# Gated linear attention into a routed expert layer on one core: fewer two-part sums, and the hand-over of PSUM banks and row gathers to the experts

## The chip, the cores and the metric

The kernel runs on one core of a Trainium2 chip. A core has TensorE (PE, matmuls; its weight loads are listed apart as PEld), VectorE (DVE), ScalarE (ACT), GpSimd (POOL) and SyncE (SP), which work beside one another and wait for each other by semaphores, and 16 DMA engines. The metric is the device time of one execution in microseconds (us). Lower is better. The kernel's arithmetic is f32, with the exception of some sums that are told of below.

## The reference

First a recurrent attention with a decay per key channel, for 4 batches, 8 heads, 768 steps, 48 channels a head. Its result, one row of 384 numbers per step and batch (3072 rows), goes to a layer of eight experts, where each row goes to the one expert with the largest logit.

```python
def _attn_ref(q, k, v, alpha):
    for t in range(S):
        state = alpha[:, :, t, :, None] * state + np.einsum('bhd,bhe->bhde', k[:, :, t], v[:, :, t])
        y[:, :, t] = np.einsum('bhd,bhde->bhe', q[:, :, t], state)

def _moe_ref(x, w_gate, w1, w2):          # x: 3072 x 384, w1: 8 x 384 x 1024, w2: 8 x 1024 x 384
    logits = x @ w_gate
    expert_idx = np.argmax(logits, axis=1)
    ...
    for e in range(E):
        lo, hi = (boundaries[e], boundaries[e + 1])
        h = np.maximum(x_sorted[lo:hi] @ w1[e], 0.0)
        y_sorted[lo:hi] = h @ w2[e]
    y = y_sorted[inv_perm]
    return (gate_w[:, None] * y).astype(np.float32)
```

## The kernel before, in words

**The attention** runs over 24 chunks: 6 stretches of 128 steps for each of 4 batches, numbered so that chunk s is stretch s // 4 of batch s % 4. The main loop (line 703) is a software pipeline with an order written out by hand: in pass i it takes the scores of chunk i, the transposes of chunk i + 1, the operands of chunk i + 2, the result rows of chunk i - 1, the gate of chunk i - 2, and the decay sums of a chunk some five ahead. Each engine works through its instructions in the order in which the program issues them.

For the decay, `logs` takes on ACT the logarithm of alpha (tile `lna`), `cums` sums it over the steps on PE by a product with a triangular matrix (tile `cum` in PSUM), and ACT takes two exponentials of the sum (`icp`, `cp`). The sum is made in one of two ways. Plain: one f32 product with `cum_m`. Two-part, where `apart(s)` holds: `logs` also scales the logarithm into an f16 tile `hi` (ACT), `low_part` puts the remainder into `lo` (DVE), and `cums` adds an f16 and an f32r product. Which pass takes a chunk's logarithm also hangs on the constant APART: from chunk APART on it is taken one pass ahead of the sum, before that in the same pass:

```python
def new_logs(i):
    return [s for j in (i, i + 1) for s in new_sums(j) if (s >= APART) == (j > i)]
```

New sums are those of chunks 4 and 5 in pass 1, 6 and 7 in pass 2, 8 in pass 3, 9 in pass 4, 10 in pass 5 and so on.

In a pass ACT's order is: `yT` (the attention's result out of PSUM), `gex` (gate), the logarithms and scalings, `kT` and for some chunks `qT` (transposed operands), `icp` and `cp`, then `xs` (rows times gate weight, out of the PSUM tile `x`), then the issue of small transfers (`dec`: decay rows of a chunk's first and last step). On POOL each pass forms the operands `kqb` (k times icp, q times cp); every fourth pass it multiplies the decay rows into the tile `er` (lines 445, 446), which PE transposes to `ep` in the next pass (457) for the state's scaling `U` (507). PE's order in a pass is scores, on every fourth pass `ep`, transposes, sum, state and value products, key-value products, rows (`x`).

**The seam.** The experts are worked off by size: places 1 to 7 in order of load, and place 0 for the first expert. Of expert 0's rows the first 256 are gathered and worked early, inside the attention's tail (`early_gather`, `early_layer1`, hidden layer in `eg["h"]`, tile `h0`); the rest, 168 at most, are a group of their own (`groups[0]`), in blocks of 128 and 40. When routing is known (`decode`, `place_experts`, DVE), the attention's pools close, the experts' pools open (line 820 on), and these follow at lines 1229 to 1239: the gather of the rest's rows (two indirect DMAs on POOL), layer 2 of the first early block, `places` (DVE: rows of places 1 to 7), the gather of place 1 (four indirect DMAs), half of layer 2 of the second early block, the transposes of the rest (`turn`), then layer 1 of the rest. `scatter` copies a block of results out of PSUM (ACT, tile `zo`, four buffers) and writes the rows by an indirect DMA on POOL.

PSUM has eight banks of 512 f32 numbers. The attention uses `y` (two banks), `tp` (two), `sA`, `sB`, `cum`, `x`. The experts have a pool `mps` of their own, opened after the attention's pool `ps` has closed: tags `pA`, `pB`, `pC`, `tp`, two buffers each.

**The experts.** Places 1 to 6 run `layer1` and `layer2` in seven products of half size (`chain`): a product goes to a bank, ACT or DVE copies or adds it out. In `layer2`, `p2` writes a `pC` bank, out of which DVE adds, and the product of the third column block goes to the next `pC` bank (line 1025).

Of the kernel before, what the change touches and what calls it, by code (L numbers as in the profile page):

```python
# [20 lines left out]
def kernel(  # L21
# [43 lines left out]
    HC = C // 2  # L65


    APART, HS = 9, 512.0
    assert NB * C == S and FB * C == F and DB * C == Dm and D <= DP


# [20 lines left out]
    cum_r = consts.tile([C, C], F32R)  # L92
    cum_h = consts.tile([C, C], F16)
    kqb = [consts.tile([C, 2, NP, 2, DP], F32, name=f"kqb{i}") for i in range(3)]
    er = consts.tile([C, NP, 2, DP], F32)

    iw = consts.tile([C, NP, D2 + E], F32)

# [133 lines left out]

    sm = ctx.enter_context(tc.tile_pool(name="moe_sm", bufs=1))
    early = ctx.enter_context(tc.tile_pool(name="early", bufs=1))
    oh_r = sm.tile([C, NT, C], F16)
    oh_c = sm.tile([C, NT, NC], F16)

# [121 lines left out]
    def weights(i, layer):  # L359
        if 0 < i < E:  # L360
            ex = nc.sync.value_load(pd["xe"][0:1, i : i + 1], min_val=0, max_val=E - 1)
            groups[i][f"w{layer}"] = fetch(ex, layer)

# [2 lines left out]

    in_order = ExitStack()  # L370
    in_order.enter_context(tc.manual_schedule())
    with tc.tile_pool(name="ld", bufs=6) as ld, \
         tc.tile_pool(name="work", bufs=2) as work, \
         tc.tile_pool(name="ps", bufs=1, space=PSUM) as ps:
        st = {s: {} for s in range(NT)}
        y = ps.tile([C, 2, 512], F32, name="y")
        decay, alpha0 = {}, {}

        def yv(g):
# [13 lines left out]

        def apart(s):

            return s >= APART or s in (5, 7)

        def logs(s):
            t = work.tile([C, Dm], F32, name="lna", bufs=4)
# [412 lines left out]
        early_layer1(FB - 1)  # L812
        d = decode(held["tok"][:], NC, "a")
        g_e = next(d)
        place_experts()
        weights(1, 1)
        _, s_e, gf_e, sf_e = next(d)
# [2 lines left out]
    spool = ctx.enter_context(tc.tile_pool(name="spool", bufs=2))  # L820
    xg_pool = ctx.enter_context(tc.tile_pool(name="moe_x", bufs=2))
    wk = ctx.enter_context(tc.tile_pool(name="moe_wk", bufs=1))
    mps = ctx.enter_context(tc.tile_pool(name="moe_ps", bufs=2, space=PSUM))

    def blocks(g, by=1):
        return [(j, min(C, -(-(g["n"] - j * C) // by) * by)) for j in range(-(-g["n"] // C))]

    def gather(g):
        g["xg"] = xg_pool.tile([C, NJ, Dm], F32, name="xg")
        for j, r in blocks(g, 16):  # L830
            nc.gpsimd.indirect_dma_start(  # L831
                out=g["xg"][:r, j, :], out_offset=None,
                in_=x_d[:, :], in_offset=bass.IndirectOffsetOnAxis(ap=g["gi"](j, r), axis=0),
            )

    def turn(g):
        g["xT"] = wk.tile([C, DB, CAP0 + 8], F32, name="xgT")
        for j, r in blocks(g):
            tp = mps.tile([C, DB, C], F32, name="tp", tag="tp")
            for a in range(DB):  # L840
                nc.tensor.transpose(tp[:, a, :r], g["xg"][:r, j, a * C : (a + 1) * C], ident[:r, :r])
            (nc.scalar.copy if j % 2 else nc.vector.tensor_copy)(g["xT"][:, :, j * C : j * C + r], tp[:, :, :r])
            if j == 1:
                yield
# [32 lines left out]
    def chain(g, terms, out, res):  # L877


        m = g["n"] // 2  # L880
        bank = {}

        def ps(n):
            bank[n] = mps.tile([C, 512], F32, name="p" + n, tag="p" + n)
            return bank[n][:, :m]

        def keep(n):
            t = wk.tile([C, CAP0 // 2], F32, name=n, bufs=2)
            nc.scalar.copy(t[:, :m], bank["A"][:, :m])  # L889
            bank[n] = t  # L890

        def p1():
            terms(ps("A"), True, "P1")
            keep("p1")

        def p2():
            terms(ps("C"), True, "P2", "R11")
            add(nc.vector, out(0, 0), bank["C"][:, :m], bank["p1"][:, :m])
            res(0, 0)

        def p7():
            terms(ps("B"), True, "P7", "R22")

        def p6():
            terms(bank["A"][:, :m], False, "P6")
            keep("u2")

        def p5():
            terms(bank["A"][:, :m], False, "P5")
            keep("u4")  # L910

        def c22():
            add(nc.vector, out(1, 1), bank["B"][:, :m], bank["u4"][:, :m])

        def p3():
            terms(bank["A"][:, :m], False, "P3", "R12")
            res(0, 1, bank["A"][:, :m])

        def p4():
            terms(bank["B"][:, :m], False, "P4", "Rd")  # L920
            add(nc.vector, out(1, 0), bank["B"][:, :m], bank["u2"][:, :m])
            res(1, 0)

        return p1, p2, p7, p6, p5, c22, p3, p4
# [69 lines left out]
    def layer2(g):  # L994
        n, m = g["n"], g["n"] // 2
        w2, h, s, t = g["w2"], g["h"], g["s2"], g["th"]
        g["zT"] = wk.tile([C, DB, CAP0 + 8], F32, name="zT")
        z = g["zT"]
        ops = {}
        for n_, (w, i) in dict(P1=(w2, 0), P2=(w2, FH), P4=(w2, FH), P3=(s, 3), P5=(s, 0), P6=(s, 1), P7=(s, 2)).items():  # L1000
            c0 = C if n_ == "P4" else 0
            for f in range(FH):
                lhs = w2[:, i + f, c0 : c0 + C] if w is w2 else s[:, i, f, :]
                rhs = {
                    "P1": h[:, f, :m], "P2": h[:, FH + f, :m], "P3": h[:, FH + f, m:n],
                    "P4": t[:, 3, f, :m], "P5": t[:, 0, f, :m], "P6": t[:, 1, f, :m], "P7": t[:, 2, f, :m],
                }[n_]
                ops.setdefault(n_, []).append((lhs, rhs))

        def terms(out, first, *names):  # L1010
            for f, (lhs, rhs) in enumerate(ops[names[0]]):
                nc.tensor.matmul(out, lhsT=lhs, rhs=rhs, start=first and f == 0, stop=True, skip_group_check=True)  # L1012

        def out(i, k):
            return z[:, i, k * m : (k + 1) * m]

        def res(i, k, at=None):
            if at is not None:
                nc.scalar.copy(out(i, k), at)

        p1, p2, p7, p6, p5, c22, p3, p4 = chain(g, terms, out, res)

        def rest(ahead, between):
            p2()
            d2 = mps.tile([C, 512], F32, name="pC", tag="pC")

            def third(fs):
                for f in fs:
                    nc.tensor.matmul(  # L1029
                        d2[:, :n], lhsT=w2[:, f, 2 * C :], rhs=h[:, f, :n], start=(f == 0), stop=(f == FB - 1),  # L1030
                    )

            third(range(FH))
            p6()
            next(between)
            third(range(FH, FB))
            ahead()
            nc.scalar.copy(z[:, 2, :n], d2[:, :n])
            next(between)
            p5()  # L1040
            next(between)
            p7()
            c22()
            p3()
            p4()

        return p1, rest
# [44 lines left out]
    def rows_layer2(g, j, fs):  # L1092

        r = min(C, g["n"] - j * C)
        if fs[0] == ready[0]:
            t = "p" + "CAB"[j]
            g["z"] = mps.tile([C, 512], F32, name=t, tag=t)
        for f in fs:
            nc.tensor.matmul(
                g["z"][:r, :Dm], lhsT=g["h"][:, f, j * C : j * C + r], rhs=g["w2"][:, f, :],  # L1100
# [3 lines left out]
    def plain(g):  # L1104

        hT = wk.tile([C, FB, CAP0], F32, name="h_sb")[:, :, :C]
        for f in range(FB):
            hp = mps.tile([C, 512], F32, name="pA", tag="pA")
            for a in range(DB):
                nc.tensor.matmul(  # L1110
                    hp[:, :C], lhsT=g["w1"][:, a, f * C : (f + 1) * C], rhs=g["xT"][:, a, :C],
                    start=(a == 0), stop=(a == DB - 1),
                )
            nc.scalar.activation(hT[:, f, :], hp[:, :C], AF.Relu)
        zp = mps.tile([C, 512], F32, name="pB", tag="pB")
        for f in range(FB):
            nc.tensor.matmul(
                zp[:, :Dm], lhsT=hT[:, f, :], rhs=g["w2"][:, f, :], start=(f == 0), stop=(f == FB - 1),
# [60 lines left out]
        pd.update(xn=xn, xi=xi, xx=xx)  # L1179
        yield  # L1180

    def cols_of(t, c0):
        return lambda j, r: t[:r, c0 + j : c0 + j + 1]

    def early_layer2(j, fs):

        if 0 in fs:
            t = "tp" if j else "pA"
            eg["z"] = mps.tile([C, DB, C], F32, name=t, tag=t).rearrange("p a c -> p (a c)")
        for f in fs:  # L1190
            nc.tensor.matmul(
                eg["z"][:, :Dm], lhsT=eg["h"][:, f, j * C : (j + 1) * C], rhs=groups[0]["w2"][:, f, :],
                start=(f == 0), stop=(f == FB - 1),
            )
        if FB - 1 in fs:
            scatter(eg, j, C, eg["z"][:, :Dm])

    def rest_layer1(g, beside):
        n = g["n"]
        g["h"] = wk.tile([C, FB, CAP0], F32, name="h_sb")  # L1200
        for f in range(FB):
            t = "p" + "CBA"[f % 3]
            hp = mps.tile([C, 512], F32, name=t, tag=t)
            for a in range(DB):
                nc.tensor.matmul(
                    hp[:, :n], lhsT=g["w1"][:, a, f * C : (f + 1) * C], rhs=g["xT"][:, a, :n],
# [8 lines left out]
    def rest_layer2(g, d):  # L1215
        n = g["n"]
        if d == 0:
            g["zT"] = wk.tile([C, DB, CAP0 + 8], F32, name="zT")
        zp = mps.tile([C, 512], F32, name="pA", tag="pA")
        for f in range(FB):  # L1220
            nc.tensor.matmul(  # L1221
                zp[:, :n], lhsT=g["w2"][:, f, d * C : (d + 1) * C], rhs=g["h"][:, f, :n], start=(f == 0), stop=(f == FB - 1),
            )
        nc.scalar.copy(g["zT"][:, d, :n], zp[:, :n])

    g0 = groups[0]
    g0["gi"], g0["si"] = cols_of(g_e, EARLY // C), cols_of(s_e, EARLY // C)

    gather(g0)
    early_layer2(0, range(FH))  # L1230
    pl = places()
    early_layer2(0, range(FH, FB))
    gp, sp = next(pl)
    for i, g in enumerate(groups[1:], 1):
        g["gi"], g["si"] = cols_of(gp, i * NJ), cols_of(sp, i * NJ)
    gather(groups[1])
    early_layer2(1, range(FH))
    for _ in turn(g0):
        pass

    def beside(i):
# [8 lines left out]
    for i, g in enumerate(groups):  # L1250
# [16 lines left out]
        if i:  # L1267
            layer1(g, beside(i), begin, last)
        else:
            rest_layer1(g, pl)  # L1270

            early_layer2(1, range(FH, FB))
            weights(1, 2)
        weights(i + 2, 1)
        if i + 2 < E:
# [54 lines left out]
    with tc.If(nx > 0):  # L1330
        with tc.For_i(0, nx, 1) as i:
# [4 lines left out]
            nc.vector.scalar_tensor_tensor(  # L1336
                m[:], in0=rc[:, 1, :], scalar=col[:], in1=tokv[:], op0=ALU.is_equal, op1=ALU.mult,
            )
            tok = mps.tile([C, 512], F32, name="pC", tag="pC")
            for s in range(NT):  # L1340
                nc.tensor.matmul(tok[:, :1], lhsT=oh_r[:, s, :], rhs=m[:, s : s + 1], start=(s == 0), stop=(s == NT - 1))
            d = decode(tok[:, :1], 1, "x", wk)
# [35 lines left out]
```

## Time and profile before

| | |
|---|---|
| runs | 398.55, 398.64, 398.83 us; median 398.64 |
| the profiled execution | 402.97 us |
| its span, first to last instruction | 401.2 us |
| PE busy | 384.8 us (96%) |
| DVE, ACT, POOL busy | 215.6, 226.5, 149.9 us |
| mean granted TensorE clock | 0.992 |
| attention's passes | to about 143 us |
| seam | about 143 to 183 us |
| places 1 to 7 | about 183 to 400 us |

The page divides the span into 40 slices of about 10 us. A digit is a busy share in tenths, and PEclk is the clock that was granted to TensorE in tenths of full speed:

```
PE   7997989999999999899999999999999999999994
PEclk9998999999999999999999999999999999999998
DMA  8999599989994313866856667866966965611311
```

In a timeline a row is: start in us, duration in us, engine, line, operation, output <- inputs, shapes, count; in brackets the time that the engine sat idle before it, and what released it. "issue" is a wait that the profile shows no releaser for. A releaser is inferred from events, and can name a neighbour of the true one.

### The profile page before, as it was taken

How to read it: one execution, taken by the hardware profiler on the slowest of the kernel's cores; microseconds unless marked ns; L12 is line 12 of the kernel's file. 1: busy time of each engine (PE TensorE's matmuls, PEld its weight loads, DVE VectorE, ACT ScalarE, POOL GpSimd, SP SyncE). 2: the span in 40 equal slices, each digit the busy share in tenths (PEclk: the TensorE clock that was granted, in tenths of full speed). 3: DMA queues.
4: the chain of work that ended last, by engine and by line, in shares of the span. 5: the costliest groups of instructions: out<-in, count | busy, mean ns of one | idle time of the engine just before them, and what ended most of it. 6: DMA issues, size and time to landing. Idle time of an engine off the chain costs nothing.

```text
span 401.2 us, 9118 instructions
## 1 busy us (share of the span) xinstructions
PE 384.8 (96%) x3390; PEld 326.6 (81%) x3390; DVE 215.6 (54%) x655; ACT 226.5 (56%) x519; POOL 149.9 (37%) x203
## 2 busy tenths in 40 slices
PE   7997989999999999899999999999999999999994
PEld 4676778888888786779979979979979979979852
DVE  5654657686666657461781582483483483561200
ACT  4666576677755441113565766666666666763640
POOL 6645536579859201447014007007008003012031
PEclk9998999999999999999999999999999999999998
DMA  8999599989994313866856667866966965611311
GB/s 166 191 199 221 117 216 202 203 177 259 258 220 143 121 60 93 332 223 159 182 170 151 181 197 171 210 197 150 227 181 147 243 196 124 191 21 55 59 57 55
DMA packets 153921, 67.44 MB, mean 168 GB/s; under 512 B 136715, under 2 KB 148098, under 8 KB 153876
## 3 DMA queue, kind: packets, MB, share of 16 engines
q1 hardware_dynamic: 148772, 57.13, 59.2%
q0 software_dynamic: 3408, 9.64, 8.2%
q8 instruction: 27, 0.44, 0.5%
q10 hardware_dynamic: 1696, 0.08, 0.3%
q14 instruction: 18, 0.15, 0.1%
HBM read 49.00 MB, written 9.58 MB: 146 GB/s over the span
## 4 chain that ended last, share of the span: by engine, by line
PE 62%; issue 22%; POOL 6%; DVE 3%; ACT 3%; DMA 3%; POOLq 1%; ACTq 0%; DVEq 0%
PE pA L947 7%; PE pC L1029 5%; PE pB L947 5%; PE sA L492 5%; PE tp L479 5%; PE pA L1012 4%; PE y L529 4%; PE x L566 3%; POOL out_dram L1059 3%; PE pC L947 2%; PE y L519 2%; PE pA L1221 2%; PE pB L1012 2%; PE tp L661 2%; PE pC L1012 2%
## 5 line engine op out<-in xcount | busy, mean ns | idle before, releaser
L1059 POOL DMA_INDIRECT out_dram<-zo,sp x25 | 26.0, 1040 | 137.7 <-ACT zo L1084 127.5
L193 DVE TENSOR_TENSOR h_sb<-pB,u 128x208 f32<-128x208 f32 (+6 forms) x56 | 20.2, 360 | 53.6 <-PE pB L947 37.3
L466 POOL TENSOR_TENSOR kqb<-k_sb,icp 128x384 f32<-128x384 f32 x23 | 23.2, 1009 | 31.7 <-PE y L540 17.2
L1029 PE MATMUL pC<-h_sb,w 128*128 128x416 f32 (+5 forms) x96 | 33.9, 496 | 0.0
L889 ACT COPY u<-pA 128x208 f32<-128x208 f32 (+6 forms) x68 | 21.1, 311 | 18.3 <-PE pA L1012 11.5
L947 PE MATMUL pA<-t,s 128*128 128x208 f32 (+6 forms) x112 | 28.8, 339 | 0.8
L492 PE MATMUL sA<-qT,kT 48*128 48x128 f32 x192 | 28.6, 291 | 0.9 <-DVE qT L483 0.9
L492 PE MATMUL sB<-qT,kT 48*128 48x128 f32 x192 | 28.6, 291 | 0.0
L947 PE MATMUL pA<-xgT,w 128*128 128x208 f32 (+6 forms) x112 | 27.7, 329 | 0.0
L492 PEld LDWEIGHTS sA<-qT,kT 48*128 48x128 f32 x192 | 23.9, 193 | 3.9 <-ACT kT L485 1.1
L479 PE MATMUL tp<-ident,kqb 128*128 128x128 f32 x192 | 26.2, 279 | 0.6 <-DVE kqb L466 0.6
L831 POOL DMA_INDIRECT xg<-x_rows,gp x25 | 23.8, 953 | 6.9 <-issue 6.5
L1029 PEld LDWEIGHTS pC<-h_sb,w 128*128 128x128 f32 x96 | 18.0, 190 | 10.3 <-issue 3.7
L566 PE MATMUL x<-iw,yT 128*64 128x104 f32 x368 | 21.6, 261 | 3.8 <-ACT xs L591 3.8
L958 ACT ACTIVATE h_sb<-h_sb 128x208 f32<-128x208 f32 (+6 forms) x28 | 10.3, 366 | 25.0 <-DVE h_sb L193 21.8
L548 ACT COPY yT<-y 128x512 f32<-128x512 f32 x24 | 14.1, 586 | 17.9 <-PE y L540 6.7
L466 POOL TENSOR_TENSOR kqb<-q_sb,cp 128x384 f32<-128x384 f32 x23 | 23.2, 1009 | 2.1 <-DMA q_sb<-in_q_dram 2.0
L492 PEld LDWEIGHTS sB<-qT,kT 48*128 48x128 f32 x192 | 23.9, 193 | 0.0
L947 PE MATMUL pB<-t,w 128*128 128x208 f32 (+6 forms) x112 | 23.8, 335 | 0.0
L479 PEld LDWEIGHTS tp<-ident,kqb 128*128 128x128 f32 x192 | 20.5, 141 | 3.5 <-issue 1.2
L947 PE MATMUL pC<-xgT,w 128*128 128x208 f32 (+6 forms) x112 | 23.1, 329 | 0.0
L500 DVE TENSOR_TENSOR dA<-sA,cmask 128x512 f32<-128x512 f32 x24 | 16.5, 688 | 10.7 <-PE sB L492 10.7
(267 smaller groups left out, 992.0 us busy)
## 6 DMA issues: line engine op xcount, KB each, us to landing
w<-in_moe_w_dram SPq DMA_DIRECT2D x14, 1536.0 KB
x_rows<-xs SPq DMA_DIRECT2D x24, 192.0 KB
v_sb<-in_v_dram SPq DMA_DIRECT2D x10, 384.0 KB
k_sb<-in_k_dram SPq DMA_DIRECT2D x9, 384.0 KB
q_sb<-in_q_dram SPq DMA_DIRECT2D x9, 384.0 KB
a_sb<-in_alpha_dram SPq DMA_DIRECT2D x7, 384.0 KB
a_sb<-in_alpha_dram SPq DMA_DIRECT2D x10, 192.0 KB
w<-in_moe_w_dram SPq DMA_DIRECT2D x6, 256.0 KB
```

The costliest lines, as they stand in the source:

```text
L193: eng.tensor_tensor(out, a, b, op=ALU.add)
L466: eng.tensor_tensor(by_half(kq[:, i]), d[n].rearrange("s (a p) d -> s a p d", a=2), d[e][:].rearrange("s (a p d) -> s a p d", a=2, p=NP), ...
L479: nc.tensor.transpose(tp[:, p, :], pair(kqb[s % 3][:, i], p), ident[:])
L492: nc.tensor.matmul(t[:, p, :], lhsT=d["kT"][r : r + D, p, :], rhs=d["qT"][r : r + D, p, :], start=True, stop=True,)
L500: nc.vector.tensor_tensor(t[:], d["sc"][i][:], cmask[:, None, :].to_broadcast([C, NP, C]), op=ALU.mult)
L566: nc.tensor.matmul(d["x"][o : o + HC, m, : D2 + E], lhsT=d["yT"][:, m // 2, m % 2, o : o + HC], rhs=iw[:, m, :], start=True, stop=True,)
L831: nc.gpsimd.indirect_dma_start(out=g["xg"][:r, j, :], out_offset=None, in_=x_d[:, :], in_offset=bass.IndirectOffsetOnAxis(ap=g["gi"](j, r) ...
L889: nc.scalar.copy(t[:, :m], bank["A"][:, :m])
L947: nc.tensor.matmul(out, lhsT=ops[n_][0], rhs=ops[n_][1], start=first and n_ == names[0], stop=True, skip_group_check=True,)
L1012: nc.tensor.matmul(out, lhsT=lhs, rhs=rhs, start=first and f == 0, stop=True, skip_group_check=True)
L1029: nc.tensor.matmul(d2[:, :n], lhsT=w2[:, f, 2 * C :], rhs=h[:, f, :n], start=(f == 0), stop=(f == FB - 1),)
L1059: ins = nc.gpsimd.indirect_dma_start(out=out[:, :], out_offset=bass.IndirectOffsetOnAxis(ap=g["si"](j, r), axis=0), in_=zo[:r], in_offset= ...
```

## The change

The diff does five things.

1. APART goes from 9 to 11, and `apart` holds for chunk 7 and from 11 on. So chunks 5, 9 and 10 are summed plainly, and the logarithms of 9 and 10 are taken in the pass of their sum, passes 4 and 5.
2. The tile `er` moves from the constants to the attention's `work` pool.
3. The rest of expert 0's rows gets a tile of its own, `xg0`, in the pool `early`, and is gathered right after the row numbers are decoded, ahead of `place_experts`.
4. The attention's PSUM pool `ps` stays open, and the experts take its banks, each name alternating strictly between two: `pA` sA and x, `pB` cum and sB, `pC` the two halves of y, `tp` the two tp. In the rest's `turn` the second block goes to a pC bank.
5. Layer 2 of the first early block is issued whole; its copy and scatter follow the gather of place 1.

```diff
-    APART, HS = 9, 512.0
+    APART, HS = 11, 512.0
...
-            return s >= APART or s in (5, 7)
+            return s >= APART or s == 7
...
+    g0 = groups[0]
+    g0["xg"] = early.tile([C, -(-g0["n"] // C), Dm], F32, name="xg0")
...
     def gather(g):
-        g["xg"] = xg_pool.tile([C, NJ, Dm], F32, name="xg")
+        if "xg" not in g:
+            g["xg"] = xg_pool.tile([C, NJ, Dm], F32, name="xg")
...
+        er = work.tile([C, NP, 2, DP], F32, name="er", bufs=1)
...
         g_e = next(d)
+        g0["gi"] = cols_of(g_e, EARLY // C)
+        gather(g0)
         place_experts()
...
-    mps = ctx.enter_context(tc.tile_pool(name="moe_ps", bufs=2, space=PSUM))
+    pairs = dict(pA=("sA", "x"), pB=("cum", "sB"), pC=(0, 1), tp=("tp", "tp"))
+    banks = {n: [] for n in pairs}
+
+    def bank(n):
+        b = banks[n]
+        if len(b) < 2:
+            t = pairs[n][len(b)]
+            if n == "pC":
+                b.append(y[:, t, :])
+            else:
+                b.append(ps.tile([C, 512], F32, name=t, bufs=2 if n == "tp" else 1)[:])
+        else:
+            b.append(b.pop(0))
+        return b[-1]
...
-    def turn(g):
+    def turn(g, second="tp"):
...
-            tp = mps.tile([C, DB, C], F32, name="tp", tag="tp")
+            tp = blocks_of(bank(second if j == 1 else "tp"))
...
         if FB - 1 in fs:
+            yield
             scatter(eg, j, C, eg["z"][:, :Dm])
+        yield
...
-    gather(g0)
-    early_layer2(0, range(FH))
+    l2 = early_layer2(0, range(FB))
+    next(l2)
     pl = places()
-    early_layer2(0, range(FH, FB))
     gp, sp = next(pl)
     for i, g in enumerate(groups[1:], 1):
         g["gi"], g["si"] = cols_of(gp, i * NJ), cols_of(sp, i * NJ)
     gather(groups[1])
-    early_layer2(1, range(FH))
-    for _ in turn(g0):
+    next(l2)
+    next(early_layer2(1, range(FH)))
+    for _ in turn(g0, "pC"):
         pass
```

The other places that used `mps` (`chain`, `layer2`, `rows_layer2`, `plain`, `rest_layer1`, `rest_layer2` and the overflow loop) now call `bank` with the same names.

## The prediction

> **What bounds the kernel now.** I read the page's shares first. TensorE (PE) is busy for 384.8 of 401.2 us, so the end moves only if PE gets less work or loses an idle or slow stretch. The row of slices says where such a stretch is: the only slice before the last with a clock below 9 is the fourth, 30 to 40 us. Windows over that slice, for PE alone, come next: busy us, granted clock, DMA share, GB/s.
>
> ```profile
> 30.00:33.00 3.00, 0.37 (x14) 0.99 0.99 200
> 33.00:36.50 3.50, 3.50 (x34) 0.52 1.26 244
> 36.50:40.00 3.50, 3.50 (x64) 1.00 1.09 214
> ```
>
> PE is idle for some 2.6 us and then runs 3.5 us at half clock. The timeline of the same stretch, engine by engine, gives the cause:
>
> ```profile
> 29.99 0.52 ACT L400 ACTIVATE lna<-a_sb 128x384 f32<-128x384 f32 x1 [2.62 <-DMA a_sb<-in_alpha_dram]
> 30.97 0.57 ACT L485 COPY kT<-tp 128x512 f32<-128x512 f32 x1
> 32.19 0.59 ACT L591 ACTIVATE xs<-x,gw 128x384 f32<-128x384 f32 x1
> 32.83 1.58 PE L566 MATMUL x<-iw,yT 128*64 128x104 f32 x16 [2.63 <-ACT xs L591]
> 31.47 1.20 POOL L446 TENSOR_TENSOR er<-er,alpha 4x384 f32<-4x384 f32 x1
> 36.36 0.41 PE L457 MATMUL ep<-ident,er 4*128 4x4 f32 x4
> ```
>
> This is pass 3. ScalarE (ACT) works in order. The log of chunk 9, asked for one pass early, waits 2.62 us for chunk 9's alpha; behind it stand kT, two exponentials and xs, which frees the PSUM bank of the next x. From 60 us on, PE's largest single waits are these, at the seam between attention and experts:
>
> ```profile
> 154.49 5.43 PE L1191 MATMUL pA<-w,h 128*128 128x384 f32 x16 [0.47 <-ACT h L665]
> 163.53 0.38 PE L841 MATMUL tp<-ident,xg 40*128 40x40 f32 x3 [0.71 <-issue]
> 164.25 1.12 PE L1205 MATMUL pC<-xgT,w 128*128 128x168 f32 x6 [0.35 <-ACT xgT L842]
> 173.98 0.48 ACT L1055 COPY zo<-tp 128x384 f32<-128x384 f32 x1 [3.12 <-PE tp L1191]
> ```
>
> After 176 us PE is busy to the tail, and no wait on a weight load appears among its waits there: what reaches 176 earlier ends earlier.
>
> **APART 9 to 11.** Chunk 9's log moves from pass 3 to pass 4, chunk 10's from pass 4 to pass 5; both, and chunk 5, go back to one f32 product.
>
> Pass 3 without the wait: kT can start when its transposes (27.06) are half done, at about 27.7; chunk 8's sum leaves PE at 28.8; two exponentials of 0.49 end at 29.8 (the gate weight is ready at 29.56); xs of 0.59 ends at 30.4. So x starts at 30.4, not 32.83, directly behind the products that end at 30.2, and there is no long idle. x and the scores then take 0.73 and 1.1 us at full clock and end at 32.3. Late next is er: GpSimd's second er product ends at 32.67, and its queue was held by chunk 5's q load, which this change leaves. So ep starts at 32.75 instead of 36.36: **3.6 us**.
>
> What the clock adds is weighed here. [...] The row shows half clock after exactly this gap. I take 3.6 and keep 2.0 as the other end.
>
> Given back: a two-part sum takes PE 0.43 us (54.86 to the next product at 55.29); an f32 product of 384 columns 0.68 (eight in 5.43, L1191). So +0.25 each. Chunk 9's is on the path, chunk 10's partly beside a wait on ACT: 0.5 for both. Chunk 5 pays 0.25 but no longer waits 0.46 for lo (18.76); it gains about 0.2 that er's q load swallows: 0. In pass 5 ACT gets a second Ln of 0.51; xs there waited 0.46 for the gate weight, so it costs 0.05 to 0.51, and I take 0.1. The three scalings (0.52, ACT) and three subtractions lo (0.56 to 1.40, VectorE) that go are not on PE's path except as said. In passes 5 and 6 some gain is lost to transfers: the DMA engines stay full to 43.7 us whatever PE does, and yT at 48.20 waited 2.34 us for a decay row, one that would now be issued into the full queues. For this I take 0.3; the ends are 0 and 2. Later passes keep their own pace of 5.1 to 6 us, and the DMA engines stood idle from 44.5 to 49.5, so loads can follow. **Early sum: 3.6 - 0.5 - 0.1 - 0.3 = 2.7 us** (ends 0.3, with the page's 2.0 and the dearer transfers, and 3.3).
>
> **The seam.** With the attention's banks kept, the first product of expert layer 2 goes to the bank sA, last read at 147.5; it no longer waits for the last relu and follows the previous product at 154.02: -0.47. If the wait comes from tracking the whole h0 tile rather than its parts, it stays: 0. The second block of the rest's rows (40 of them) goes to a pC bank and need not wait for the copy of the first: -0.71, with layer 1's own wait for both copies ending together at 0.05 after VectorE's copy. Against this, tp banks now strictly alternate: place 1's first block must take the bank of z, so it waits for the zo copy (ends 174.46) where it ran at 173.78. Its copy then ends later, and the third block waits for it: blocks end about 0.3 us later than now. **Late sum: -0.47 - 0.71 + 0.3 = -0.9** (ends -0.2 and -1.2).
>
> **Moves I cost at nothing.** The rest's two gathers (0.99 and 0.90, GpSimd) start about 153.9, when their indices are cast (153.59 plus the 0.3 the early gather took), instead of 154.86. Their rows are wanted at 162.0, so 1 us sooner buys nothing, and GpSimd's queue is empty there (19.56 us idle before). [...] I take 0.
>
> Place 1's four gathers (about 1.25 apart) go ahead of z's scatter: from 158.8, when VectorE has their indices (158.51), instead of 162.16. The scatter slides from 160.83 to about 163.9; behind it on GpSimd stands nothing until 174.74, and zo has four buffers. Place 1's rows are wanted at 173.8 and were not waited for: 0. SP's queue keeps its order, and its weight fetch at 156.37 hangs on VectorE's chain, which is not moved. er's new place and the tile xg0 add no instruction.
>
> **The sum.** 2.7 + 0.9 = 3.6 us off the profiled execution, 402.97 us (span 401.2): 399.4. The runs' median is 398.64, 1.1% below; in the same ratio 3.55, so **395.1 us**. Unprofiled transfers may leave a shorter alpha wait, which the range covers.
>
> **Rivals.**
> 1. *The forecast* (0.58): 395.1; its own range 394.0 to 396.3.
> 2. *The transfers take the early gain* (0.22). For: the DMA share is above 1 from 31 to 44 us, decay rows took 4.7 us to land at 25.49, and POOL's er at 57.75 waited 4.11 us for transfers. Against: 5 us of idle DMA after 44.5. Early 0.7 left, late 0.9: 1.6, so 397.0.
> 3. *Nothing to speak of* (0.11): the log waits for its load one pass later, or PE waits for er so long that the clock still falls, and the early banks wait as before. For: er ends only 0.3 after the new scores. Against: alpha 9 landed at 29.95, before pass 4. About 398.4.
> 4. *Slower: the two pC banks are one tile, y* (0.09). If dependencies are kept for y as a whole, layer 2's third-column product (L1029), which takes the second half while VectorE still adds out of the first, must wait for that add in each of the six chained experts. The add at 203.12 ends at 203.49, and L1029 started at 202.73:
>
> ```profile
> 202.73 2.96 PE L1029 MATMUL pC<-h_sb,w 128*128 128x416 f32 x8
> 203.12 0.37 DVE L193 TENSOR_TENSOR zT<-pC,p 128x208 f32<-128x208 f32 x1
> ```
>
> That is 0.65 to 1.0 us each (0.76 with a restart of 0.15 to 0.25), about 0.95 x 6 = 5.7: 400.8. It decides from 0.59 per expert on (3.55 / 6). Against it: parts of one xg tile are filled by gathers that do not wait for one another (1.25 us apart).
>
> **Range and chances.** This kernel's measurement tells about 0.2% (0.8 us) from no change. Low end 393.9, where early gives its 3.3 and late its 1.2 with a little over; high end 398.6, which takes in rivals 2 and 3 and leaves out rival 4. Faster by over 0.2% (below 397.84): 0.58 and most of 0.22, 0.78. Within: 0.12. Slower (above 399.44): 0.10.
>
> **What would show it.** In the after profile: a PEclk of 9 in the fourth slice; one Ln, not two, in pass 3, and x right behind the products; ep near 32.7 with PE waiting on POOL's er for 0.3 to 0.5; three f32 sums more and three two-part ones fewer; the first layer-2 product of the experts at the heels of the last early one; layer 1 of the rest about 1.2 sooner after it; zo ahead of place 1's first transposes. Wrong would be: a new ACT wait for alpha in pass 4, a wait of L1029 on DVE's add, or passes 5 to 8 (yT's waits on decay rows) that swallow the 3 us.

## The result, and the profile after

The changed kernel takes 401.20 us (median of 21 runs, 400.17 to 403.12). The kernel before, run beside it on the same chip, takes 400.95 us (21 runs, 398.50 to 403.36). The ratio is 1.0021, with a 95% interval of 1.0000 to 1.0042: no gain, at best equal. The forecast was 395.1 us, with a range up to 398.6.

The runs of before lie in two groups with nothing between 399.12 and 400.70: nine around 398.83 (median) and twelve around 401.73. The three that were shown ahead of the prediction were all of the lower group; the profiled execution, 402.97 us with a mean clock of 0.992, was of the upper one. The changed kernel's runs make one group. So it is 2.4 us above before's short runs and 0.5 us below its long ones. Both the groups and these 2.4 us have to be explained.

The profile after has a span of 399.9 us in an execution of 401.60. First its rows of slices (tenths), and the group of the product that rival 4 spoke of: the line of before (L1029), then that of after (L1055). A group's line has line, engine, operation, shapes, count | busy us, mean ns | idle us before it, and what ended it.

```profile
PE   7999999999999999999999999999999999999994
PEclk9999999999999999999999999999999999999999
DMA  8999999999994218769739449758757856701311
...
L1029 PE MATMUL pC<-h_sb,w 128*128 128x416 f32 (+5 forms) x96 | 33.9, 496 | 0.0
...
L1055 PE MATMUL y<-h_sb,w 128*128 128x416 f32 (+5 forms) x96 | 34.5, 502 | 3.7 <-DVE zT L192 3.7
```

The fourth slice is at full clock, as forecast. The group had no idle time before it; now it has 3.7 us, all put down to DVE's add. Windows over the early stretch (busy us, granted clock, DMA share, GB/s):

```profile
30.00:33.00 3.00, 2.81 (x56) 1.00 0.86 176
33.00:36.50 3.50, 2.87 (x36) 1.00 1.24 226
36.50:40.00 3.50, 3.50 (x69) 1.00 0.93 199
```

The timeline of pass 3 there:

```profile
28.33 0.59 ACT L502 COPY kT<-tp 128x512 f32<-128x512 f32 x1 [0.25 <-PE tp L496]
30.23 0.58 ACT L608 ACTIVATE xs<-x,gw 128x384 f32<-128x384 f32 x1
30.87 0.93 PE L583 MATMUL x<-iw,yT 128*64 128x104 f32 x16
30.56 1.00 POOL L483 TENSOR_TENSOR kqb<-q_sb,cp 128x384 f32<-128x384 f32 x1 [1.57 <-DMA q_sb<-in_q_dram]
33.63 0.41 PE L474 MATMUL ep<-ident,er 4*128 4x4 f32 x4 [0.74 <-POOL er L463]
```

In this pass ACT no longer waits for alpha, and x starts 0.1 us after PE's products before it end (30.78). The seam, with its timeline:

```profile
149.05 5.33 PE L1212 MATMUL sA<-w,h 128*128 128x384 f32 x16
157.98 1.09 PE L1227 MATMUL y<-xgT,w 128*128 128x168 f32 x6 [0.39 <-ACT xgT L868]
167.67 0.48 ACT L1081 COPY zo<-tp 128x384 f32<-128x384 f32 x1 [3.12 <-PE tp L1212]
168.21 0.87 PE L867 MATMUL tp<-ident,xg 128*128 128x128 f32 x6 [0.57 <-ACT zo L1081]
169.47 0.85 PE L867 MATMUL tp<-ident,xg 128*128 128x128 f32 x6 [0.39 <-DVE xgT L868]
```

The first layer-2 product starts without a wait. Place 1's transposes wait for zo, as the prediction said of the alternating tp banks. And the experts, first PE's waits from 180 us on (us in total, times, longest), then the timeline around the first of the six:

```profile
PE y L1055 <- DVE zT L192: 3.7, 6, 0.6
PE y L1124 <- ACT h_sb L986: 0.3, 1, 0.3
```

```profile
194.57 1.83 PE L1038 MATMUL y<-h_sb,w 128*128 128x208 f32 x8
196.62 0.37 DVE L192 TENSOR_TENSOR zT<-y,p 128x208 f32<-128x208 f32 x1
197.04 3.06 PE L1055 MATMUL y<-h_sb,w 128*128 128x416 f32 x8 [0.65 <-DVE zT L192]
```

The add reads one half of y until 196.99; the product into the other half starts at 197.04. This happens once in each of places 1 to 6.

Where the time went is best read in three stages. The bounds are starts of PE's products in the view by source line: the last early layer-1 product, and the experts' first.

| profiled execution | early, to last early product | seam | experts, to the end of the span | span |
|---|---|---|---|---|
| before (402.97, a long run) | 153.6 | 29.3 | 218.3 | 401.2 |
| before (399.38, a short run, from the first experiment) | 150.0 | 29.3 | 218.4 | 397.7 |
| after | 148.8 | 28.4 | 222.7 | 399.9 |

Against the short run: -1.2 - 0.9 + 4.3 = +2.2, near the 2.4 between the medians. Against the long one: -4.8 - 0.9 + 4.4 = -1.3.

### The profile page after: what moved, and what is told of

Its sections match the earlier page's. It is cut to its first block, busy times and chain, and to the rows that moved or that the text cites. A ratio compares the mean times of both kernels' runs of the same rounds, so it can differ in the third digit from the quotient of the medians.

```text
span 399.9 us, 9108 instructions
## 1 busy us (share of the span) xinstructions
PE 384.2 (96%) x3390; PEld 325.5 (81%) x3390; DVE 215.4 (54%) x652; ACT 225.1 (56%) x516; POOL 147.9 (37%) x203
## 4 chain that ended last, share of the span: by engine, by line
PE 67%; issue 15%; DMA 4%; ACT 3%; DVE 3%; POOL 3%; SPq 2%; ACTq 1%; POOLq 0%; DVEq 0%
PE y L1055 7%; PE sA L509 4%; PE tp L496 4%; PE y L546 4%; PE x L973 4%; PE sA L973 4%; PE sA L1038 4%; PE x L583 3%; PE y L973 3%; PE cum L973 3%; PE sB L973 3%; PE x L1038 3%; DMA q_sb<-in_q_dram 3%; PE y L536 2%; SPq L405 2%
## 5 line engine op out<-in xcount | busy, mean ns | idle before, releaser
L1085 POOL DMA_INDIRECT out_dram<-zo,sp x25 | 24.8, 991 | 143.2 <-ACT zo L1110 132.2
L1055 PE MATMUL y<-h_sb,w 128*128 128x416 f32 (+5 forms) x96 | 34.5, 502 | 3.7 <-DVE zT L192 3.7
L1055 PEld LDWEIGHTS y<-h_sb,w 128*128 128x128 f32 x96 | 17.6, 190 | 15.8 <-DVE zT L192 5.5
L509 PE MATMUL sA<-qT,kT 48*128 48x128 f32 x192 | 27.7, 285 | 0.9 <-DVE qT L500 0.9
L192 DVE TENSOR_TENSOR h_sb<-cum,u 128x208 f32<-128x208 f32 (+6 forms) x28 | 10.1, 359 | 27.3 <-PE cum L973 20.8
L192 DVE TENSOR_TENSOR h_sb<-sB,u 128x208 f32<-128x208 f32 (+6 forms) x28 | 10.1, 359 | 26.1 <-PE sB L973 18.7
L973 PE MATMUL y<-xgT,w 128*128 128x208 f32 (+6 forms) x112 | 23.1, 329 | 0.0
L195 DVE TENSOR_TENSOR th<-h_sb,th 128x208 f32<-128x208 f32 (+5 forms) x48 | 17.3, 361 | 7.9 <-ACT h_sb L986 7.9
L1110 ACT COPY zo<-zr 128x768 uint16<-128x768 uint16 (+2 forms) x20 | 19.9, 1052 | 0.0
L973 PEld LDWEIGHTS y<-xgT,w 128*128 128x128 f32 x112 | 19.2, 190 | 0.0
```

Source lines behind the costliest of these rows:

```text
L192: eng.tensor_tensor(out, a, b, op=ALU.add)
L195: eng.tensor_tensor(out, a, b, op=ALU.subtract)
L509: nc.tensor.matmul(t[:, p, :], lhsT=d["kT"][r : r + D, p, :], rhs=d["qT"][r : r + D, p, :], start=True, stop=True,)
L973: nc.tensor.matmul(out, lhsT=ops[n_][0], rhs=ops[n_][1], start=first and n_ == names[0], stop=True, skip_group_check=True,)
L1055: nc.tensor.matmul(d2[:, :n], lhsT=w2[:, f, 2 * C :], rhs=h[:, f, :n], start=(f == 0), stop=(f == FB - 1),)
L1085: ins = nc.gpsimd.indirect_dma_start(out=out[:, :], out_offset=bass.IndirectOffsetOnAxis(ap=g["si"](j, r), axis=0), in_=zo[:r], in_offset= ...
```

## The experiments: what lengthens the experts

Theory 1: the six waits come from the two pC banks being one tile, as rival 4 of the prediction has it; and before's two groups of runs are the early stretch with and without the half clock (the granted clock of about 0.5 after PE's gap in pass 3). The rivals are that the experts are longer through the moved order or the way banks alternate, and that the groups have another source. The kernels were run in three sets, each beside 23 runs of before: its medians are 400.93, 401.23 and 401.38 us. In each set, runs of before with a granted clock of 0.996 or more make a group; these medians (399.72, 399.14, 400.02) are used below as "before at full clock".

**The pC pair on tiles of its own.** The changed kernel, with y's halves given to pB instead:

```diff
-    pairs = dict(pA=("sA", "x"), pB=("cum", "sB"), pC=(0, 1), tp=("tp", "tp"))
+    pairs = dict(pA=("cum", "sB"), pB=(0, 1), pC=("sA", "x"), tp=("tp", "tp"))
...
-            if n == "pC":
+            if n == "pB":
```

> The changed kernel with one edit: the experts' pC pair lies in two tiles of its own (sA and x), and pB has the two halves of y. Theory 1 (the six waits of L1055 for VectorE's add at L192, 0.59 to 0.65 us each, and the issue time around them, come from the two pC banks being one tile): the waits are gone, P2 to L1055 is again 1.66 us and not 2.47, and the time falls by 6 x 0.75 = some 4.5 us against the changed kernel, to about 397 (396 to 398); ratio to before 0.985 to 0.995. A new small wait may show where pB's two halves are used by turns. Rival (the experts are longer for another reason: strict alternation of the banks, weights arriving later): the waits may move but the stretch from L973 to the end stays near 222.7 us and the time near 401.

Measured: 411.94 us (410.95 to 412.66, 6 runs), ratio 1.0261 (1.0217 to 1.0305). The time forecast was far off, but the waits moved with the tile. PE's waits from 177 us on:

```profile
PE y L973 <- DVE h_sb L192: 12.1, 14, 1.5
PE sA L1124 <- ACT h_sb L986: 0.3, 1, 0.3
```

L1055 waits no more and starts 1.67 us after p2 (197.49 to 199.16, against 2.47 in after), as before. But pB is used more often by turns than pC: 14 waits of L973, 0.86 us each, and the experts take 233.7 us. "A new small wait" was the wrong expectation; y is dear wherever its halves are turned.

**The kernel before, with one tile for pC.** Nothing else is changed; one tile of two banks, its halves by turns:

```diff
+    duo = []
+    def mtile(t):
+        if t != "pC":
+            return mps.tile([C, 512], F32, name=t, tag=t)
+        if not duo:
+            two = mps.tile([C, 2, 512], F32, name=t, tag=t, bufs=1)
+            duo.extend((two[:, 0, :], two[:, 1, :]))
+        duo.append(duo.pop(0))
+        return duo[-1]
...
-            d2 = mps.tile([C, 512], F32, name="pC", tag="pC")
+            d2 = mtile("pC")
...
```

> The kernel before with one edit: the two pC banks of the experts are two halves of one tile, used by turns; pA, pB and tp stay as they are. Theory 1 (two halves of one tile are waited for as one, whatever else stands around them): six waits of L1029's third block for VectorE's add at L193, 0.6 us each, and the stretch of the experts 4 to 5 us longer than 218.3; time some 4.5 us above before's on the same chip (ratio 1.009 to 1.013). Rival (the experts' extra time comes from the moved order or from the banks' history in the attention, not from the tile): no waits, ratio 1.00.

Measured: 406.19 us, ratio 1.0133 (1.0088 to 1.0177). PE's waits from 180 us on:

```profile
PE pC L1039 <- DVE zT L193: 3.7, 6, 0.6
PE pC L1109 <- ACT h_sb L970: 0.3, 1, 0.3
```

The same six waits, 3.7 us, in a kernel whose order, other banks and early part are before's; its stages are 150.7, 29.3 and 222.9. This shows the cause: two halves of one tile, used by turns, are waited for as one.

**y's halves in two pairs.** The changed kernel, with each half of y paired with a tp bank, so that both halves are seldom in use at once. The banks are the same eight:

```diff
-    pairs = dict(pA=("sA", "x"), pB=("cum", "sB"), pC=(0, 1), tp=("tp", "tp"))
+    pairs = dict(pA=("sA", "x"), pB=("cum", "sB"), pC=("tp", 0), tp=("tp", 1))
...
-            if n == "pC":
+            if not isinstance(t, str):
...
```

> The changed kernel with one edit: the halves of y go to two pairs that are seldom busy together: pC is one tp bank and one half of y, tp the other tp bank and the other half. Theory 1: the six waits of L1055 are gone, because the add reads one half while the other half is idle; experts near 218.4 us, seam near 28.4 us, so below the first part alone (396.8) by the seam's 0.9: 395.3 to 396.8. Rival (any use of y in the experts costs, through transposes of the next place that meet the add): single waits at L867 or L1055, time 397 to 400.

Measured: **395.71 us** (395.52 to 396.67, 6 runs), ratio 0.9863 (0.9825 to 0.9901). It beats both kernels. PE's waits from 170 us on have no L1055:

```profile
PE tp L867 <- DVE xgT L868: 0.4, 1, 0.4
PE tp L1124 <- ACT h_sb L986: 0.3, 1, 0.3
```

Its stages are 149.2, 28.3 and 217.4: the seam's gain is kept. The experts are even 1.0 us shorter than before's. By the starts of L1055 and L1029, 0.7 of this lies ahead of the first one (19.08 us after the first product, against 19.81); why layer 1 of place 1 runs smoother there was not tried.

## The experiments: the early part

**The kernel before, unchanged,** for the clock of each run and a second profile.

> The kernel before, unchanged, to see the span and the granted clock of each of its runs. Theory 1 (the 21 runs of before are of two kinds because the early wait of pass 3 for the chunk-9/10 decays, and the half clock it brings, occurs in some runs and not in others): its runs fall into two groups some 3 us apart, near 398.6 and near 401.7, the long ones with a mean granted clock near 0.992 and the short ones nearer 0.998 or above. Rival (the spread comes from elsewhere: the experts, the chip, the transfers): the clock does not follow the time, or the profiled execution of a short run still has the 2.6 us gap ahead of ep. Ratio to before 1.00 either way.

Measured: nine of twelve runs at 398.89 to 400.87 us with a clock of 0.997 to 1.000, and three at 402.84 to 403.79 with 0.986 to 0.989. The groups are there, with the clock as said; the profile is of a short run. Its row of x in pass 3 and its windows:

```profile
32.86 0.93 PE L566 MATMUL x<-iw,yT 128*64 128x104 f32 x16 [1.74 <-ACT xs L591]
```

```profile
30.00:33.00 3.00, 1.26 (x33) 1.00 1.11 220
33.00:36.50 3.50, 3.50 (x46) 1.00 1.20 240
```

Alpha lands no sooner (the log starts at 30.02, 29.99 in the long run). PE reaches the gap 0.9 us later (in pass 2 its sum waited 0.82 us and its x 0.53, both for ACT); the gap is 1.74 us and not 2.63, the clock stays, and the early part is 3.6 us shorter.

**Work put into the gap.** The kernel before, with three products into a bank that nobody reads:

```diff
+            if i == 3:
+                fill = ps.tile([C, NP, C], F32, name="sA")
+                for _ in range(3):
+                    nc.tensor.matmul(fill[:], lhsT=ident[:], rhs=st[i]["qT"][:], start=True, stop=True)
             do(rows, i - 1)
```

> The kernel before with added work and nothing removed: in pass 3 three 128x512 products into the bank sA, which nobody reads, ahead of the products x that wait for ScalarE. Theory 1 (before's runs are of two kinds because PE's gap of 2.6 us ahead of x drops the granted clock, and a gap of 1.7 us does not): the gap is filled, so no run loses the clock: all runs near 398.6 to 399.6 with a granted clock of 0.996 or more, none above 401; x still waits for ScalarE's xs until about 32.8 us. Rival (the long runs are long for another reason, and the low clock goes with them by chance): two groups again, a median near 400.9.

Measured: 400.25 us (398.96 to 400.95, 12 runs), ratio 0.9982 (0.9953 to 1.0011). No run has a clock below 0.996 and none is above 401, while 14 of the 23 runs of before beside it had 0.984 to 0.993. So the gap makes the long runs. The filler was too long:

```profile
30.50 2.84 PE L775 MATMUL sA<-qT,ident 128*128 128x512 f32 x6
33.28 0.93 PE L566 MATMUL x<-iw,yT 128*64 128x104 f32 x16
```

xs ended at 32.47 and x waited for the filler to 33.28, which is most of the 1.1 us by which these runs lie above before at full clock. A shorter filler was not tried.

**The first part of the change alone.** The kernel before with

```diff
-    APART, HS = 9, 512.0
+    APART, HS = 11, 512.0
...
-            return s >= APART or s in (5, 7)
+            return s >= APART or s == 7
```

> The kernel before with the first part of the change alone: two-part sums from chunk 11 on and for chunk 7, nothing moved behind it. Theory 1: no wait of ScalarE for the decays of chunks 9/10 in pass 3, PE's gap ahead of ep under 1 us, granted clock 0.997 or above, seam (30.4 us) and experts (218.3 us) as in before; so the early 4.8 us alone: a span near 396.4 where the profiled before had 401.2, time 397 to 398.5, in one group. Rival 1 (the early gain is given back further on, at the seam or in the experts): early part shorter but the time near 400 to 401. Rival 2 (the early gain belongs to a kind of run and not to this edit): two groups of times again, as in before.

Measured: 396.81 us (396.49 to 397.96, 6 runs), ratio 0.9886 (0.9844 to 0.9928), a little under the time expected, clock 0.997 to 1.000 in every run, stages 148.2, 29.3 and 218.7. Against before at full clock it is 2.9 us.

**The change without this part** (APART 9 again, `s in (5, 7)`):

> The changed kernel with the first part undone: two-part sums again from chunk 9 on and for chunks 5 and 7; the rest's tile, the banks and place 1's order stay. Theory 1: the early wait of before is back (ep near 36 us, in some or all of the runs), seam 0.9 us shorter than before, experts 4.4 us longer by the six waits of L1055: 0.9 and 4.4 make 3.5 us more than before, 402 to 406. Rival (the experts' extra time comes from the early part, through the order in which transfers or weights arrive): experts near 218 us and a time below before's.

Measured: 404.37 us (403.20 to 407.72, 12 runs), ratio 1.0082 (1.0046 to 1.0118). The stages are 153.4, 28.4 and 223.2. Its x in pass 3 by the timeline, and PE's wait in the experts:

```profile
32.94 1.65 PE L583 MATMUL x<-iw,yT 128*64 128x104 f32 x16 [2.79 <-ACT xs L608]
```

```profile
PE y L1055 <- DVE zT L192: 3.7, 6, 0.6
```

Five of its twelve runs have the low clock. The seven at full clock have 403.94, 4.2 us above before's, where seam and experts make -0.9 + 4.8 = 3.9. So the parts add up; the experts' extra time does not hang on the early part.

**Saved operations or shifted logs?** The first part does two things: it drops three scalings, three subtractions and three two-part sums, and it takes two logarithms a pass later. Two kernels do one each. First the savings alone, early logs kept:

```diff
-            return s >= APART or s in (5, 7)
+            return s >= 11 or s == 7
...
-                if s >= APART:
+                if s >= APART and apart(s):
                     low_part(s)
```

> The kernel before with the cheaper sums of the change's first part but without its shift in time: chunks 5, 9 and 10 get one plain f32 sum, yet the logs of chunks 9 and 10 stay a pass early, where ScalarE waits for their decays. Theory 1 (the gain of the first part is the wait that leaves ScalarE's order, not the operations saved): the wait of about 2 us for the decays stays in pass 3, PE's gap ahead of x is 1.2 to 2.2 us (0.52 us less than before for the missing half-precision copy), early part 0.5 us shorter than before at equal clock; fewer or no runs with the dropped clock; median 398 to 400.5. Rival (the operations saved are what counts): 396.8 like the first part alone.

Measured: 397.47 us (396.49 to 401.74, 12 runs), ratio 0.9922 (0.9889 to 0.9956). At full clock 397.22, 1.9 us below before at full clock. Two runs have a clock of 0.989 and 0.991, at 401.74 and 400.99. The profile fell on the first of these; windows of 2 us:

```profile
30.00:32.00 2.00, 0.21 (x10) 1.00 0.93 191
32.00:34.00 2.00, 1.74 (x22) 0.74 1.15 220
34.00:36.00 2.00, 2.00 (x19) 0.50 1.04 207
36.00:38.00 2.00, 2.00 (x9) 0.50 1.12 262
38.00:40.00 2.00, 2.00 (x20) 0.55 1.10 219
```

The wait for alpha stays (2.59 us), the gap is 2.06 us, and the clock falls. From these windows PE was at half clock for 2 x 2 x (0.26 + 0.50 + 0.50 + 0.45) = 6.84 us. Half of it, 3.4 us, is the author's estimate of what PE lost by this. The same kernel once more, for a profile at full clock:

> The cheaper sums with the logs of chunks 9 and 10 left early, once more, for a profile at full clock (its first profile lost the clock in pass 3). Theory 1: x of pass 3 near 32.3 us as before, 0.9 later than with the first part whole, and of this only some 0.4 left at the end of the early part, the rest having been made good in passes 4 to 6, where the next products wait for k and q in any case. Rival: the 0.9 us stay to the end, and the time of its full-clock runs near 397.1 has another source.

Measured: 398.23 us (397.98 to 402.25, 10 runs), ratio 0.9926 (0.9895 to 0.9957); eight runs at full clock have 398.13, again 1.9 us below before's. The profile fell on a low clock again, so where the later x is made good in the full-clock runs stays open.

Then the shift alone, two-part sums kept:

```diff
-            return [s for j in (i, i + 1) for s in new_sums(j) if (s >= APART) == (j > i)]
+            return [s for j in (i, i + 1) for s in new_sums(j) if (s >= 11) == (j > i)]
...
-            do(transposes, i + 1, *[s for s in new_sums(i) if apart(s) and s < APART])
+            do(transposes, i + 1, *[s for s in new_sums(i) if apart(s) and s < 11])
...
-                if s >= APART:
+                if s >= 11:
                     low_part(s)
```

> The kernel before with the time shift of the change's first part and none of its savings: chunks 5, 7, 9 and 10 keep their two-part sums, but the logs of chunks 9 and 10 come in their own pass, behind their decays' arrival. Together with the kernel that saves the operations and keeps the early logs (fast runs near 397.1) it tells the two apart. Theory 1, as it stands after that run (the half clock goes with the gap, but of the 2 us that remain between runs at full clock, the saved operations make about 1.6 and the shift 0.4): no wait for the decays in pass 3, no low clock, all runs in one group at 398 to 399. Rival (the shift alone is enough, the savings only made the same slack in another way): 396.5 to 397.3.

Measured: 398.36 us (397.90 to 400.67, 12 runs), ratio 0.9933 (0.9907 to 0.9958), no low clock. The absolute time is in theory 1's range, but before was slower in this set too (400.02 us at full clock, 399.14 in the set of the savings), and against that the gain is 1.7 us and not theory 1's 0.4. That the gain is smaller than the whole part's goes with PE's sums now waiting for `lo`, 1.6 us in all where before's short run has 0.2:

```profile
PE cum L420 <- DVE lo L410: 1.6, 3, 0.7
```

So either half alone brings 1.7 to 1.9 us at full clock, both together 2.9; my first theory, that only the shift counts, and its successor, that it hardly counts, both fell. Only the shift takes away every low clock that was seen; the savings alone leave a few.

## Why the prediction was wrong

**The step that failed** is a term that the sum put at nothing. Its "what reaches 176 earlier ends earlier" takes it that the experts run on the new banks as they did before, and so that the two halves of y are two banks to the program. They were waited for as one, six times, and the experts took 4.3 us more. The prediction had this as rival 4, with the price worked out, and gave it 0.09 on the ground that gathers into parts of one SBUF tile do not wait for one another. That was another kind of access (transfers that write, none that reads), and it carried no evidence for a product that follows a read. The price was nearly right. L1055 comes 0.84 us later in each place (155.68 us from the first to the sixth start, 151.48 in before's short run, over five places): six times 0.84 is 5.0 us, where the rival said 0.95 and 5.7. The restart of 0.15 to 0.25 us that it counted is shown by no run: in after the product starts 0.05 us after the add ends. The experts show 4.3 and not 5.0 because the first stretch of place 1 got some 0.7 shorter. That rival 4's 400.8 us is within 0.4 of the measured 401.20 is luck in part: it has an early gain of 2.7 us where 1.0 to 1.2 came, and 5.7 us in the experts where 4.3 came, and the two errors nearly cancel.

**The base of the sum** was wrong too. The sum was made against a long run, whose 2.63 us gap and half clock it took away, and was then scaled to the median of three runs of the short group, which has a mean clock of 0.996 or more wherever it is on record. What remains to be gained from those is less: 1.2 us in the early part by the profiles, where the sum had 2.7. Against the long run it is 4.8. The term "early" was thus mis-sized in both directions; over before's runs together the first part alone gives 4.1 us (400.93 to 396.81). The low end of the early sum is also mis-added: 2.0 - 0.5 - 0.1 - 2 is -0.6, not 0.3; no other number was built on it. That the median of before moved from 398.64 to 400.95 with more runs is the same mixture.

**Pass 3** went as described: kT and xs without the wait, x at 30.87 (30.4 said). But ep came at 33.63 and not 32.75: POOL's operands waited 1.57 us for chunk 5's q load, and er came 0.9 us late. "3.6 us" at ep was 2.7.

**The clock.** The forecast went by the row, half clock after the 2.63 us gap. The other end, 2.0 us at ep, was the author's estimate for a clock that stays after such a gap, and no run shows it. What the runs showed in its place: in before's short run the gap was 1.74 us and the clock stayed at 1.00, and against that run the early part gained 1.2 us. Nor did every gap cost the clock. Gaps of 2.63 us (before), 2.79 (the change without its first part), 2.06 and 1.85 us (the two profiles of the savings alone) were followed by half clock. Gaps of 1.74 us (before's short run) and 2.20 us (the kernel with one tile for pC) were not: the clock is 1.00 in every window from 24 to 42 us. The length of the gap alone does not decide, and what does was not shown. By the windows the half clock lasted some 3.4 us in before, 2 x (3 x 0.01 + 3.5 x 0.48), and 6.8 us in the other three; why it lasted longer there stays open.

**The seam** was right: -0.9 said, -0.9 measured (29.3 to 28.4). The early banks gave 0.64 (0.47 said), the blocks of the rest 0.87 (0.71 said), and the tp alternation cost about 0.6 (0.3 said).

**The moves at no cost** were right. The rest's gathers, now at 149.06 and 150.35 beside VectorE's run of small operations, took 0.99 and 0.90 us, as they had in before at 154.86 and 156.15 beside the same run; place 1's rows and the late scatter held up nothing.

**The early part of the whole change** gained less than the first part alone. By the medians it is 1.0 us (2.4 = -1.0 - 0.9 + 4.3), and 1.5 with the split pairs, against 2.9; by the profiles the three are 1.2, 0.8 and 1.8. That transfers took the difference (rival 2) is not shown. The sum had them late in passes 5 and 6. In pass 7 of after POOL's er waits for the decay rows `dec`:

```profile
POOL er L462 <- DMA dec<-cp: 2.5, 1, 2.5
```

This wait is 3.7 us with the split pairs, but it is 2.6 us in before's short run too, and 2.1 with the shift alone, so the other parts of the change do not bring it. Pass 3's ep starts at 33.63 in after and at 33.35 with the first part alone; the next ep at 55.54 and 54.86. What makes this difference was not settled; putting `er` back among the constants, the one part that touches this tile, was not tried.

With the failed step mended, by the split pairs, the kernel takes 395.71 us. That this is near 395.1 is luck in part: against before at full clock the gain is 3.4 us, of which the early part has 1.5 and not 2.7, and the experts give 1.0 that the sum did not have.

## What to carry to other kernels

Two halves of one tile, used by turns as a double buffer, were waited for as one buffer here (six waits, 3.7 us in all, in the kernel before with one tile for pC): give each bank its own tile, or pair halves so that both are never in use at once, and look at the reader that stands before the next write before counting on the second half. Before a sum is made against a profiled execution, find out whether the runs that it will be compared with had the same stall; a stall that costs the clock can come and go from run to run, as it did here (a low mean clock in 11, 14 and 12 of 23 runs). An idle gap of about 2 us in front of dense matmuls can cost more afterwards than it lasts: a gap of 2.06 us was followed by 6.84 us of half clock here. Work that nobody reads, put into the gap, kept the clock in all twelve runs here, but made 0.8 us too long it gave the gain back; whether a filler shorter than the gap wins was not tried.

## What the runs showed of the hardware

The kernel before is faster or slower by some 2.1 to 2.9 us from run to run with the same data: in the three sets, 11, 14 and 12 of its 23 runs had a mean clock of 0.993 or less. In the profile of a long run the granted clock is 0.52 from 33 to 36.5 us, behind a PE gap of 2.63 us in pass 3; in that of a short run it is 1.00 there, behind a gap of 1.74 us. With work put into the gap, none of twelve runs had a mean clock below 0.996. The length of the gap alone does not decide it: a gap of 1.85 us was followed by half clock, while one of 2.20 us in another kernel was not. Once fallen, the clock came back after some 3.4 us in one profile and 6.8 us in three. By the author's estimate from its windows (half of 6.84 us), the 2.06 us gap of the kernel with early logs and cheap sums cost up to 3.4 us more than itself.
